# Softcap attention with a maxout expert layer: early loads in longer rows, reciprocals spread within the quad, multiplies ahead of casts

## The chip, the cores and the metric

The kernel runs on one core of a Trainium2 chip. The metric is the device time of one execution in microseconds (us). Medians are over all runs of a kernel. Ratios and intervals use fast runs.

Words used throughout: a *group* is three head pairs, the unit in which q, k and v are loaded; a *quad* is two head pairs, one turn `t` of the main loop; `i` counts head pairs, so quad `t` holds `i = 2t` and `2t + 1`. There are 48 head pairs, 24 quads and 16 groups. *Fillers* are matmuls of the expert layer which the loop hands out between the attention's instructions, a fixed number at each place.

## The reference, cut to what matters

```python
scores = q @ k^T / 8                       # 8 x 12 heads, 448 rows, 64 columns
scores = cap * tanh(scores / cap)          # cap = 30
attn   = softmax(scores)
x      = (attn @ v), heads side by side    # 3584 x 768
out    = maximum(x @ w1, x @ w2) @ w_out   # 1024 hidden columns
```

## The kernel before

`maximum(a, b) = relu(a - b) + b`, so the kernel builds `wd = w1 - w2` and `M = w2 @ w_out` (called `wm`) once, on TensorE, and computes `relu(x wd) w_out + x M`. Softmax needs no maximum because the scores are capped; each quad's sums are gathered at the end, inverted, and spread over the partitions by two DMAs, and the product with v is multiplied by them afterwards. That is the loop, for quad `t`:

```python
def pv(t, ab):                  # products with v; for ab = 1 also the sums
    ...
    nc.vector.tensor_copy(U[t][:, ab, :], ps[:, :S])
    if ab:
        nc.vector.tensor_copy(st, ss[:, :S])
        nc.sync.dma_start(out=sums[t], in_=st...)          # 7 KB
def invert(t):
    nc.vector.reciprocal(r, sums[t])
    nc.sync.dma_start(out=recd[t], in_=r)                  # 7 KB, to DRAM
def spread(t):
    for h in range(2):
        nc.sync.dma_start(out=rec[t][64*h : 64*h+64], in_=recd[t]... broadcast)   # 2 x 224 KB
def normalize(t, ab, eng=nc.gpsimd):
    eng.tensor_mul(xT[...], U[t][:, ab, :], rec[t][:, ab, :])
def cross(g):                   # groups 4 to 15: transposes q and k of a group
    nc.sync.dma_start_transpose(out=qkT_of(g)..., in_=kqf[g % 2]...)
```

All of these DMAs, and every load of q, k and v, are issued by SP (SyncE), one after the other. All multiplies and, but for most of group 0, all casts to bf16 run on GpSimd (POOL), one after the other. The order in a quad, for `t > 4`:

```python
for t in range(NQ):
    scores(t + 1, 0); ex(t, 3); ...
    spread(t - 2)                        # quad t-2's reciprocals, written in quad t-1
    extra(i)                             # loads, casts and cross of this point
    scores(t + 1, 1); ...; pv(t, 0)
    ...
    normalize(t - 2, 0); normalize(t - 2, 1)
    scores(t + 1, 2); ...
    invert(t - 1)
    extra(i + 1)                         # among others q of the odd groups
    scores(t + 1, 3); ...; pv(t, 1)      # sums of quad t
```

Of the kernel before, what the change touches and what calls it, by code (L numbers as in the profile page):

```python
# [10 lines left out]
def kernel(  # L11
# [11 lines left out]
    nc = tc.nc  # L23
# [78 lines left out]
    def rows(t, b, h0, h1):  # L102

        return t[b, h0:h1, :, :].rearrange("h (r j) d -> (h r) (j d)", j=R7)

    def raw_of(g, what):
        if (g, what) not in raw:
            raw[g, what] = stage.tile([P, 2 * L * NJ * D + (2 * L if what == "q" else L) * D], f32, name=what + "r")
        t = raw[g, what]
        m = t[:, : 2 * L * NJ * D].rearrange("p (h c) -> p h c", c=NJ * D)  # L110
        l = t[:, 2 * L * NJ * D :].rearrange("p (h d) -> p h d", d=D)
        return t, m, l

    def load(g, what, n0=0, n1=L):
        b, p = divmod(g * L, NP)
        h0, h1 = 2 * (p + n0), 2 * (p + n1)
        src = {"k": k, "q": q, "v": v}[what]
        t, m, l = raw_of(g, what)
        if g < NT and what == "v":

            x = rows(src, b, h0, h1).rearrange("(h r) c -> r h c", r=64)
            for a in range(2):
                nc.sync.dma_start(
                    out=m[64 * a : 64 * a + 64, 2 * n0 : 2 * n1, :], in_=x[:, :, NJ * D * a : NJ * D * (a + 1)]
                )
            for par in range(2):
                nc.sync.dma_start(
                    out=l[64 * par : 64 * par + 64, n0:n1, :], in_=x[:, par::2, 2 * NJ * D :]
                )
            return  # L130
        if g < NT:
            nc.sync.dma_start(
                out=t[:, n0 * S : n1 * S].rearrange("p (n c) -> p n c", c=S),
                in_=rows(src, b, h0, h1).rearrange("(n p) c -> p n c", p=P),
            )
            return
        nc.sync.dma_start(
            out=m[:, 2 * n0 : 2 * n1, :],
            in_=src[b, h0:h1, 0 : NJ * P, :].rearrange("h (p j) d -> p h (j d)", j=NJ),
        )  # L140
        if what == "q":
            nc.sync.dma_start(
                out=l[half(b), 2 * n0 : 2 * n1, :],
                in_=src[b, h0:h1, NJ * P : S, :].rearrange("h p d -> p h d"),
            )
        else:
            for par in range(2):
                nc.sync.dma_start(
                    out=l[64 * par : 64 * par + 64, n0:n1, :],
                    in_=src[b, h0 + par : h1 : 2, NJ * P : S, :].rearrange("h p d -> p h d"),  # L150
                )

    def cast(eng, g, what, n0=0, n1=L):

        b = g * L // NP
        x, m, l = raw_of(g, what)
        if what == "v":
            eng.tensor_copy(  # L158
                vp[g % 2][:, 2 * n0 : 2 * n1, :, :].rearrange("p h j d -> p h (j d)"), m[:, 2 * n0 : 2 * n1, :]
            )  # L160
            for par in range(2):
                r = slice(64 * par, 64 * par + 64)
                eng.tensor_copy(vl[g % 2][r, n0:n1, r], l[r, n0:n1, :])
            return
        if g < NT:

            x = x[:, n0 * S : n1 * S].rearrange("p (n c) -> p n c", c=S)
            if what == "q":
                eng.tensor_copy(flat(g)[:, n0:n1, Q0 : Q0 + S], x)
                return  # L170
            eng.tensor_copy(flat(g)[:, n0:n1, : NJ * P], x[:, :, : NJ * P])
            for par in range(2):
                r = slice(64 * par, 64 * par + 64)
                eng.tensor_copy(kf[g % 2][r, n0:n1, 3, r], x[r, :, NJ * P :])
            return
        o = b % 2 if what == "q" else 0
        t = (kf if what == "k" else qf)[g % 2]
        eng.tensor_copy(  # L178
            t[:, n0:n1, o : o + NJ, :].rearrange("p n j (h d) -> p n h j d", h=2),
            m[:, 2 * n0 : 2 * n1, :].rearrange("p (n h) (j d) -> p n h j d", h=2, d=D),  # L180
        )
        if what == "q":
            eng.tensor_copy(
                t[half(b), n0:n1, 3 * (1 - o), :],
                l[half(b), 2 * n0 : 2 * n1, :].rearrange("p (n h) d -> p n (h d)", h=2),
            )
        else:
            for par in range(2):
                r = slice(64 * par, 64 * par + 64)
                eng.tensor_copy(t[r, n0:n1, 3, r], l[r, n0:n1, :])  # L190
# [15 lines left out]
    def load_w2(c):  # L206
        nc.gpsimd.dma_start(out=w2b[:, c, :], in_=moe_w2[c * P : (c + 1) * P, :])
# [117 lines left out]
    def pv(t, ab):  # L325
# [21 lines left out]
                    nc.tensor.matmul(ss[32 * m : 32 * m + 32, :S], ones, x, start=False, stop=(j == nj - 1))  # L347
        nc.tensor.matmul(ps[:, :S], vl[g % 2][:, n, :], expo[t, 2][:, ab, :], start=False, stop=True)  # L348
        if ab == 0:
            U[t] = upool.tile([P, 2, S], f32, name="u", bufs=3)  # L350
        nc.vector.tensor_copy(U[t][:, ab, :], ps[:, :S])  # L351
        if ab:
            st = upool.tile([P, S], f32, name="st", bufs=1)
# [85 lines left out]
    def F(n):  # L439
        while n > 0 and fill_q:  # L440
            try:
                next(fill_q[0])
                n -= 1
            except StopIteration:
                fill_q.pop(0)
# [6 lines left out]
    def at(i, f, *a):  # L452
        todo[i].append((f, a))

    for g in range(2, NL):
        if g < NT:
            e = 0 if g == 2 else 1
            at(3 * g - 6 + e, load, g, "k")
            at(3 * g - 6 + e, load, g, "q")
            at(3 * g - 4 + e, load, g, "v")  # L460
            at(3 * g - 4, cast, nc.gpsimd, g, "k")
            at(3 * g - 4, cast, nc.gpsimd, g, "q")
            at(3 * g - 2, cast, nc.gpsimd, g, "v")
        else:
            e = 3 * g - g % 2
            at(e - 8, load, g, "k")
            at(e - 8 + g % 2, load, g, "q")
            at(e - 6, cast, nc.gpsimd, g, "k")
            at(e - 6, cast, nc.gpsimd, g, "q")
            at(e - 4, cross, g)  # L470
            at(e - 4, load, g, "v")
            at(e - 2, cast, nc.gpsimd, g, "v")
    at(1, load, 1, "v")
    at(2, cast, nc.gpsimd, 1, "v")
    for c, i in enumerate((3, 3, 4, 5, 6, 7)):
        todo[i].insert(c if i == 3 else 0, (load_w1, (c,)))
    MS = 3

    fill_const(nc.vector, 0)
    load(0, "k", 0, 1)  # L480
# [3 lines left out]
    load(1, "k")  # L484
    load(1, "q")
    load(0, "v")
    cast(nc.vector, 0, "k", 0, 1)
    cast(nc.gpsimd, 0, "q", 0, 1)
    fill_const(nc.gpsimd, 1)
    transposes(0)  # L490
    cast(nc.vector, 0, "k", 1, L)
    cast(nc.vector, 0, "q", 1, L)
# [7 lines left out]
    ex(0, 2)  # L500
    scores(0, 3)
    transposes(2)
    cast(nc.vector, 0, "v")
    cast(nc.gpsimd, 1, "k")
    cast(nc.gpsimd, 1, "q")
    for f in range(0, FC, 2):
        load_wo(f)
    for c in range(3):
        load_w2(c)
    for c in range(3, KC):  # L510
        load_w2(c)

    def weights(i):
# [9 lines left out]
    for t in range(NQ):  # L523
        i = 2 * t
        more = t + 1 < NQ
        more8 = 1 if t >= 8 and more else 0
        weights(i)
        if t % 3 == 2 and t > 2:
            fill_q.append(moe(t // 3 - 1))
        if more:  # L530
            scores(t + 1, 0)
        ex(t, 3)
        F(2)
        add(t, 0, 1)
        F(2)
        if i + 3 < NT * L:
            transposes(i + 3)
        F(5 + more8 if more else 0)
        if t > 4:
            spread(t - 2)  # L540
        extra(i)
        F(6 if more else 3)
        if more:
            scores(t + 1, 1)
            ex(t + 1, 0)
        pv(t, 0)
        F(8 + more8)
        F(3 if more else 0)
        if MS < i <= MS + KC:
            subtract(i - MS - 1)  # L550
        if t > 4:
            normalize(t - 2, 0)
            normalize(t - 2, 1)
        if more:
            scores(t + 1, 2)
            ex(t + 1, 1)
        weights(i + 1)
        if i + 4 < NT * L:
            transposes(i + 4)
        F(2 + more8 if more else 0)  # L560
        add(t, 1, 0)
        F(4 if more else 2)
        add(t, 1, 1)
        F(2 if more else 0)
        if t > 4:
            invert(t - 1)
        elif t > 1:
            spread(t - 2)
        extra(i + 1)
        F(3 + more8 if more else 0)  # L570
        if more:
            scores(t + 1, 3)
            ex(t + 1, 2)
        pv(t, 1)
        F(4)
        if more:
            add(t + 1, 0, 0)
        F(3 if more else 0)
        if 0 < t < 5:
            invert(t - 1)  # L580
        if 1 < t < 5:
            normalize(t - 2, 0)
            normalize(t - 2, 1)
        if MS < i + 1 <= MS + KC:
            subtract(i - MS)
    F(6)
    spread(NQ - 2)
    F(10)
    invert(NQ - 1)
    F(16)  # L590
    spread(NQ - 1)
# [40 lines left out]
```

## Time and profile before

| | before |
|---|---|
| median of three runs | 379.54 us (375.2 to 382.1) |
| span of the profiled run | 379.2 us |
| busy | PE 349.0, ACT 281.8, DVE 200.6, POOL 150.1 us |
| quad 0 ends at | 28.2 us |
| quads 1 to 7 | 93.8 us |
| quads 8 to 22 | 195.4 us, 12.2 to 13.4 each but one of 16.5 |
| last quad and what follows | 61.8 us |

The end of a quad is read from the copy of its sums, `st`, on VectorE in the order of time. The prediction below shows the lines of single quads. SP's own waits are listed below, with one of PE's. Columns: who waited, for whom, us in total, how often, the longest.

```profile
SPq L371 <- DMA rec_d<-rec_s: 31.4, 14, 4.4
PE s L295 <- DMA qkT<-kqf: 2.3, 2, 1.9
```

Line 371 is the spread. It waits until the reciprocals have landed in DRAM, and it waits on SP: while it does, nothing else is issued.

### The profile page before, as it was taken

What the parts mean: (1) busy time and instruction counts of PE and PEld (TensorE: products, weight loads), DVE (VectorE), ACT (ScalarE), POOL (GpSimd) and SP (SyncE); (2) the same over time, 40 slices, a digit from 0 to 9 for tenths busy, and PEclk for the clock granted to TensorE, in tenths of its full rate; (3) what the DMA queues carried; (4) which work ended last, traced back from release to release, by engine and by line L of the source; (5) the groups of instructions that cost most, each with busy time, mean ns of one, the idle gap of its engine ahead of it and who ended that gap; (6) DMA issues with size and microseconds to landing.
All of it is one profiled execution on the core that took longest, in us unless ns stands there. A gap on an engine that the chain in (4) does not pass through costs nothing.

```text
span 379.2 us, 6549 instructions
## 1 busy us (share of the span) xinstructions
PE 349.0 (92%) x2492; PEld 168.2 (44%) x2492; DVE 200.6 (53%) x348; ACT 281.8 (74%) x265; POOL 150.1 (40%) x188
## 2 busy tenths in 40 slices
PE   3677986898999999999999999999989999999996
PEld 2223443443444444444444454434434444555563
DVE  4223473567665676455745654557448556633421
ACT  4999986697999989998898899889958897000000
POOL 3734135637554445444562456243644302420000
PEclk9997898999999999999999999999989999999999
DMA  7999999996788987999698959896988132422022
GB/s 251 263 209 220 274 284 223 227 193 139 215 212 221 213 232 203 223 234 255 177 213 208 251 163 250 232 242 165 216 217 213 51 91 105 122 80 95 2 83 84
DMA packets 104464, 71.56 MB, mean 189 GB/s; under 512 B 58224, under 2 KB 99440, under 8 KB 104432
## 3 DMA queue, kind: packets, MB, share of 16 engines
q1 hardware_dynamic: 102480, 67.99, 71.1%
q0 software_dynamic: 1952, 3.15, 4.5%
q8 instruction: 19, 0.31, 0.4%
q14 instruction: 13, 0.11, 0.1%
HBM read 53.48 MB, written 11.18 MB: 171 GB/s over the span
## 4 chain that ended last, share of the span: by engine, by line
PE 65%; DMA 19%; DVE 5%; SPq 4%; ACT 3%; issue 2%; POOL 1%; POOLq 0%; DVEq 0%; ACTq 0%
PE mm L396 17%; PE mm L411 16%; PE mm L408 12%; PE pv L334 6%; DMA qkT<-kqf 6%; PE s L295 6%; DMA qr<-in_q_dram 6%; DMA vr<-in_v_dram 4%; DMA rec_b<-rec_d 3%; PE pv L348 3%; PE ss L347 2%; PE s L290 1%; DVE u L351 1%; ACT expo L303 1%; ACT tanh L296 1%
## 5 line engine op out<-in xcount | busy, mean ns | idle before, releaser
L296 ACT ACTIVATE tanh<-s 128x896 bf16<-128x896 f32 x144 | 124.3, 915 | 32.5 <-PE s L295 31.1
L303 ACT ACTIVATE expo<-tanh 128x1792 bf16<-128x1792 bf16 (+1 forms) x96 | 144.9, 1510 | 0.1
L383 POOL TENSOR_TENSOR xT<-u,rec_b 128x448 bf16<-128x448 f32 x48 | 58.4, 1238 | 101.1 <-DMA rec_b<-rec_d 81.2
L411 PE MATMUL mm<-wo_sb,gT 128*128 128x384 bf16 x448 | 86.8, 330 | 0.0
L396 PE MATMUL mm<-xT,wd_sb 128*128 128x448 bf16 x384 | 79.1, 354 | 2.7 <-POOL xT L383 1.3
L351 DVE COPY u<-pv 128x448 f32<-128x448 f32 x48 | 29.9, 624 | 91.0 <-PE pv L348 78.3
L408 PE MATMUL mm<-wm_sb,xT 128*128 128x384 bf16 x336 | 66.6, 326 | 0.2 <-DVE gT L400 0.2
L411 PEld LDWEIGHTS <-gT 128*128 128x128 bf16 x448 | 43.6, 99 | 31.1 <-issue 3.6
L415 DVE COPY osb<-mm 128x384 f32<-128x384 f32 x56 | 31.1, 555 | 46.3 <-PE mm L411 46.0
L396 PEld LDWEIGHTS <-wd_sb 128*128 128x128 bf16 x384 | 37.2, 98 | 38.4 <-issue 5.9
L295 PE MATMUL s<-qkT 64*128 64x448 bf16 x288 | 43.2, 371 | 11.1 <-ACT tanh L298 3.4
L400 DVE TENSOR_SCALAR gT<-mm 128x448 bf16<-128x448 f32 x64 | 39.1, 616 | 16.8 <-PE mm L396 16.6
L408 PEld LDWEIGHTS <-xT 128*128 128x128 bf16 x336 | 32.5, 98 | 23.3 <-issue 1.9
L334 PE MATMUL pv<-expo,vp 128*64 128x448 bf16 x288 | 37.5, 370 | 0.0
L158 POOL CAST vp<-vr 128x1152 bf16<-128x1152 f32 x15 | 18.0, 1201 | 46.8 <-DMA vr<-in_v_dram 43.5
L321 DVE TENSOR_TENSOR esum<-esum,expo 128x896 bf16<-128x896 bf16 x38 | 29.9, 787 | 1.5
L319 DVE TENSOR_TENSOR esum<-expo 128x896 bf16<-128x896 bf16 x38 | 26.6, 699 | 0.0
L295 PEld LDWEIGHTS <-qkT 64*128 64x128 bf16 x288 | 9.4, 95 | 36.8 <-issue 28.7
L298 ACT ACTIVATE tanh<-s 128x896 bf16<-128x896 f32 x24 | 22.0, 917 | 4.4 <-PE s L290 3.9
L334 PEld LDWEIGHTS <-vp 128*64 128x64 bf16 x288 | 12.4, 110 | 21.3 <-issue 15.2
L232 PE MATMUL mm<-wo_sb,w2T 128*128 128x384 bf16 x96 | 19.1, 334 | 1.4 <-DVE qkT L264 1.4
L178 POOL CAST kqf<-qr 128x1152 bf16<-128x1152 f32 x12 | 14.5, 1207 | 9.6 <-DMA qr<-in_q_dram 9.4
(56 smaller groups left out, 227.7 us busy)
## 6 DMA issues: line engine op xcount, KB each, us to landing
rec_b<-rec_d SPq DMA_DIRECT2D x48, 224.0 KB
kr<-in_k_dram SPq DMA_DIRECT2D x12, 576.0 KB
qr<-in_q_dram SPq DMA_DIRECT2D x12, 576.0 KB
vr<-in_v_dram SPq DMA_DIRECT2D x12, 576.0 KB
out_dram<-osb SPq DMA_DIRECT2D x17, 384.0 KB
out_dram<-osb SPq DMA_DIRECT2D x22, 192.0 KB
osb<-in_moe_w_dram SPq DMA_DIRECT2D x6, 512.0 KB
vr<-in_v_dram SPq DMA_DIRECT2D x8, 288.0 KB
```

What stands on the lines that cost most here:

```text
L295: nc.tensor.matmul(s[:, h, :S], k0[r, j * P : (j + 1) * P], qTn[r, :])
L296: nc.scalar.activation(tanh[t, p][:, 2 * m : 2 * m + 2, :], s[:, :, :S], AF.Tanh, scale=scale / cap)
L303: nc.scalar.activation(expo[t, p], tanh[t, p][:, 0:n, :], AF.Exp, scale=float(cap))
L321: nc.vector.tensor_add(d, d, e_of(t, ab, 0 if ab else 2))
L334: nc.tensor.matmul(ps[r, :S], vp[g % 2][:, 2 * n + h, j, :], e_of(t, ab, j)[:, h, :], start=(j == 0), stop=False)
L351: nc.vector.tensor_copy(U[t][:, ab, :], ps[:, :S])
L383: eng.tensor_mul(xT[b // 2][:, hp, cs], U[t][:, ab, :], rec[t][:, ab, :])
L396: nc.tensor.matmul(ps[:, :S], wd_sb[:, c, f * P : (f + 1) * P], x[:, c, cs], start=(c == 0), stop=(c == KC - 1))
L400: nc.vector.tensor_relu(g[:, f, cs], ps[:, :S])
L408: nc.tensor.matmul(ps[:, : DM // 2], x[:, c, ts], wm_sb[:, c, hs], start=(c == 0), stop=False)
L411: nc.tensor.matmul(ps[:, : DM // 2], g[:, f, ts], wo_sb[:, f, hs], start=False, stop=(f == FC - 1))
L415: nc.vector.tensor_copy(osb[:, hs], ps[:, : DM // 2])
```

## The change

Its intent: fill the holes of the first 98 us by loading in larger rows and in a better order, let the weights' product M and the second stage begin sooner, and free the U buffers sooner by spreading and multiplying as early as possible.

```diff
-        if g < NT and what == "v":            # v of groups 0 to 3: 4 DMAs with rows of 768 and 256 bytes
-            ... (removed; v now loads like q and k, rows of 1792 bytes, and the cast places the pieces)
-            U[t] = upool.tile([P, 2, S], f32, name="u", bufs=3)
+            U[t] = upool.tile([P, 2, S], f32, name="u", bufs=4)
 ...                                            # loads of the groups from 4 on
-            at(e - 8 + g % 2, load, g, "q")
+        at(e - 8, load, g, "q")
 ...                                            # early loads: one table of places; w2's first two
 ...                                            # chunks at the start; MS = 3 becomes 2
-        if t > 4:
-            spread(t - 2)
+        if t > 3:
+            normalize(t - 2, 0)
+            normalize(t - 2, 1)
         extra(i)
 ...
-        if t > 4:
-            normalize(t - 2, 0)
-            normalize(t - 2, 1)
 ...
+        if t == 4:
+            fill_q.append(moe(0))
 ...
+        if t > 2:
             invert(t - 1)
 ...
+        if t > 2:
+            spread(t - 1)
         pv(t, 1)
 ...                                            # fillers: 40 a quad instead of 44 up to quad 7, then 48 as before
```

More of the change, by code (lines that the diff above doesn't have):

```diff
@@ L118, in load @@
         t, m, l = raw_of(g, what)
-        if g < NT and what == "v":
-            x = rows(src, b, h0, h1).rearrange("(h r) c -> r h c", r=64)
-            for a in range(2):
-                nc.sync.dma_start(
-                    out=m[64 * a : 64 * a + 64, 2 * n0 : 2 * n1, :], in_=x[:, :, NJ * D * a : NJ * D * (a + 1)]
-                )
-            for par in range(2):
-                nc.sync.dma_start(
-                    out=l[64 * par : 64 * par + 64, n0:n1, :], in_=x[:, par::2, 2 * NJ * D :]
-                )
-            return
         if g < NT:
@@ L156, in cast @@
         x, m, l = raw_of(g, what)
+        if what == "v" and g < NT:
+            x = x[:, : L * S].rearrange("p (n c) -> p n c", c=S)
+            for h in range(2):
+                r = slice(64 * h, 64 * h + 64)
+                for a in range(2):
+                    eng.tensor_copy(
+                        vp[g % 2][64 * a : 64 * a + 64, h::2, :, :].rearrange("p n j d -> p n (j d)"),
+                        x[r, :, NJ * D * a : NJ * D * (a + 1)],
+                    )
+                eng.tensor_copy(vl[g % 2][r, :, r], x[r, :, 2 * NJ * D :])
+            return
         if what == "v":
@@ L453, in at @@
         todo[i].append((f, a))
-    for g in range(2, NL):
-        if g < NT:
-            e = 0 if g == 2 else 1
-            at(3 * g - 6 + e, load, g, "k")
-            at(3 * g - 6 + e, load, g, "q")
-            at(3 * g - 4 + e, load, g, "v")
-            at(3 * g - 4, cast, nc.gpsimd, g, "k")
-            at(3 * g - 4, cast, nc.gpsimd, g, "q")
-            at(3 * g - 2, cast, nc.gpsimd, g, "v")
-        else:
-            e = 3 * g - g % 2
-            at(e - 8, load, g, "k")
-            at(e - 8 + g % 2, load, g, "q")
-            at(e - 6, cast, nc.gpsimd, g, "k")
-            at(e - 6, cast, nc.gpsimd, g, "q")
-            at(e - 4, cross, g)
-            at(e - 4, load, g, "v")
-            at(e - 2, cast, nc.gpsimd, g, "v")
-    at(1, load, 1, "v")
-    at(2, cast, nc.gpsimd, 1, "v")
-    for c, i in enumerate((3, 3, 4, 5, 6, 7)):
-        todo[i].insert(c if i == 3 else 0, (load_w1, (c,)))
-    MS = 3
+    for g in range(NT, NL):
+        e = 3 * g - g % 2
+        at(e - 4, cross, g)
+        at(e - 8, load, g, "k")
+        at(e - 8, load, g, "q")
+        at(e - 4, load, g, "v")
+        at(e - 6, cast, nc.gpsimd, g, "k")
+        at(e - 6, cast, nc.gpsimd, g, "q")
+        at(e - 2, cast, nc.gpsimd, g, "v")
+    early = {
+        1: [(load, (1, "v"))],
+        2: [(load, (3, "k")), (load, (3, "q")), (load_w1, (0,))],
+        3: [(load_w1, (1,)), (load_w1, (2,)), (load, (2, "v"))],
+        4: [(load_w1, (3,))],
+        5: [(load_w1, (4,)), (load, (3, "v"))],
+        6: [(load_w1, (5,))],
+    }
+    for i, what in ((2, "2k"), (2, "2q"), (2, "1v"), (4, "2v"), (5, "3k"), (5, "3q"), (6, "3v")):
+        early[i].append((cast, (nc.gpsimd, int(what[0]), what[1])))
+    for i, x in early.items():
+        todo[i] += x
+    MS = 2
     fill_const(nc.vector, 0)
@@ L486 @@
     load(0, "v")
+    load(2, "k")
+    load(2, "q")
     cast(nc.vector, 0, "k", 0, 1)
@@ L489 @@
     fill_const(nc.gpsimd, 1)
+    load_w2(0)
+    load_w2(1)
     transposes(0)
@@ L502 @@
     transposes(2)
-    cast(nc.vector, 0, "v")
     cast(nc.gpsimd, 1, "k")
@@ L507 @@
         load_wo(f)
-    for c in range(3):
-        load_w2(c)
-    for c in range(3, KC):
+    for c in range(2, KC):
         load_w2(c)
@@ L527 @@
         weights(i)
-        if t % 3 == 2 and t > 2:
+        if t % 3 == 2 and t > 5:
             fill_q.append(moe(t // 3 - 1))
@@ L537 @@
             transposes(i + 3)
-        F(5 + more8 if more else 0)
-        if t > 4:
-            spread(t - 2)
+        if t == 0:
+            cast(nc.vector, 0, "v")
+        F(4 + more8 if more else 0)
+        if t > 3:
+            normalize(t - 2, 0)
+            normalize(t - 2, 1)
         extra(i)
-        F(6 if more else 3)
+        F(5 + 2 * more8 if more else 3)
         if more:
@@ L546 @@
         pv(t, 0)
-        F(8 + more8)
+        F(7 + 2 * more8)
         F(3 if more else 0)
-        if MS < i <= MS + KC:
-            subtract(i - MS - 1)
-        if t > 4:
-            normalize(t - 2, 0)
-            normalize(t - 2, 1)
+        if 3 <= i < 3 + KC:
+            subtract(i - 3)
         if more:
@@ L561 @@
         add(t, 1, 0)
-        F(4 if more else 2)
+        F(4 + more8 if more else 2)
         add(t, 1, 1)
         F(2 if more else 0)
-        if t > 4:
+        if 1 < t < 4:
+            spread(t - 2)
+        if t > 2:
             invert(t - 1)
-        elif t > 1:
-            spread(t - 2)
         extra(i + 1)
-        F(3 + more8 if more else 0)
+        F(2 + more8 if more else 0)
         if more:
@@ L578 @@
         F(3 if more else 0)
-        if 0 < t < 5:
+        if 0 < t < 3:
             invert(t - 1)
-        if 1 < t < 5:
+        if 1 < t < 4:
             normalize(t - 2, 0)
             normalize(t - 2, 1)
-        if MS < i + 1 <= MS + KC:
-            subtract(i - MS)
-    F(6)
-    spread(NQ - 2)
-    F(10)
+        if 3 <= i + 1 < 3 + KC:
+            subtract(i - 2)
+    F(16)
     invert(NQ - 1)
```

## The prediction

> **What bounds the kernel now.** I read the page first, then busy time by stage, then the end of every quad (a quad is one turn of the main loop, two head pairs; it ends with the copy of the softmax sums, `st`), then the orders of time of the engines where a quad was long.
>
> ```profile
> PE 349.0 (92%) x2492; PEld 168.2 (44%) x2492; DVE 200.6 (53%) x348; ACT 281.8 (74%) x265; POOL 150.1 (40%) x188
> PE   3677986898999999999999999999989999999996
> ACT  4999986697999989998898899889958897000000
> ```
>
> TensorE looks like the bound, and from the tenth slice on it is. But the first nine slices hold holes, and ScalarE runs out long before the end: the last sixth of the span is matmuls alone (the expert layer of the last two batches). Two bounds, then: ScalarE's tanh and exp pace the front, TensorE the back. ScalarE needs 281.8 us for 24 quads, so 11.7 us a quad.
>
> The stretches are cut at the ends of quads 0, 2, 5 and 7, around quad 20, and at the last quad. Columns: stretch, length, busy PE, PEld, DVE, ACT, POOL, clock, DMA share, GB/s.
>
> ```profile
> 0.00:28.20 28.20, 16.79 (x193) 7.30 (x194) 9.31 (x28) 21.74 (x21) 12.75 (x28) 1.00 1.00 241
> 28.20:53.20 25.00, 20.76 (x240) 9.99 (x238) 10.52 (x19) 24.70 (x24) 8.98 (x14) 0.86 1.03 263
> 53.20:98.40 45.20, 37.81 (x332) 18.28 (x330) 27.79 (x44) 34.47 (x34) 21.99 (x26) 0.96 0.91 202
> 98.40:122.00 23.60, 23.60 (x159) 11.12 (x157) 13.54 (x26) 22.81 (x22) 14.02 (x17) 1.00 0.81 205
> 122.00:275.00 153.00, 151.90 (x985) 70.72 (x983) 90.53 (x156) 140.71 (x134) 71.36 (x86) 1.00 0.89 219
> 275.00:292.00 17.00, 15.15 (x86) 6.60 (x85) 10.06 (x16) 12.29 (x12) 6.99 (x7) 0.90 0.89 225
> 324.00:379.20 55.20, 51.46 (x301) 29.25 (x299) 19.30 (x34) 0.00 (x0) 6.68 (x6) 0.99 0.23 75
> ```
>
> In 28 to 53 us ScalarE is full (24.7 of 25). In 53 to 98 it lacks 10.7 us, and TensorE 7.4: neither bound holds there, so that is where time can be won. The `st` copies start at 28.2, 41.3, 53.2, 70.5, 83.9, 98.4, 110.4 and 122.0: quads 1 to 7 took 13.1, 11.8, 17.3, 13.4, 14.6, 12.0 and 11.6 us.
>
> Quad 3, the worst, in order of time (start, length, engine, line, operation, count, idle time before it and what ended that):
>
> ```profile
> 51.45 2.12 SPq L371 DMA_DIRECT2D rec_b<-rec_d  x2
> 61.08 2.22 POOL L383 TENSOR_TENSOR xT<-u,rec_b 128x448 bf16<-128x448 f32 x2 [7.60 <-DMA rec_b<-rec_d]
> 63.33 0.62 DVE L351 COPY u<-pv 128x448 f32<-128x448 f32 x1 [5.60 <-POOL xT L383]
> 64.47 0.90 PE L262 MATMUL mm<-ident,kqf 64*64 64x64 bf16 x26 [3.66 <-DVE wm_sb L237]
> 67.98 1.73 ACT L296 ACTIVATE tanh<-s 128x896 bf16<-128x896 f32 x2 [4.26 <-PE s L295]
> ```
>
> The spread reciprocals of quad 0 were issued at 51.45 behind the k and q loads of two groups, and the multiply that needs them began at 61.08. Only then was the first of three U buffers free, so VectorE's copy waited 5.60 us; behind it, in VectorE's order, stood the eviction of a weight product, so TensorE waited 3.66 us and ScalarE 4.26.
>
> One late quad is odd, quad 20 (275.2 to 291.7, 16.5 us; its neighbours 12.2 and 13.4):
>
> ```profile
> 277.61 0.55 PE L295 MATMUL s<-qkT 64*128 64x448 bf16 x4 [1.85 <-DMA qkT<-kqf]
> ```
>
> A transposing DMA came late; the clock then fell (0.90 over 275 to 292).
>
> **What the Trainium skill says.** "Perfetto Trace Analysis", Identifying the Most-Contended Engine, warns that matmul occupancy does not tell how close to the limit the engine is. The trace agrees: in 98 to 122 PE is busy 23.60 of 23.60, though with ScalarE busy 22.81 the pace there is ScalarE's. So I take TensorE's need from long runs in the chain of waits: 48 products of line 396 in 9.08 us (0.189 each), six of line 408 in 0.97 (0.162).
>
> "DMA: Bandwidth & Descriptors", Queues, rings and completion order: on each DMA engine descriptors are consumed in ring order. The trace agrees: the 448 KB of `rec_b` issued at 51.45 took 8.61 us in the chain of waits.
>
> The same page, Rules for kernel authors, advises against two transfers to disjoint partition halves and for one 128-partition transfer. The trace shows the price on the queue: the four pieces of the first v took SP 2.51 + 2.00 us to issue, a whole k 0.40 to 0.56.
>
> "TensorE: Matmul & The Clock Gate", Part 1, says the clock halves after an idle window of about 3.4 us. Here the clock averaged 0.86 in 28 to 53 us; but a gap of 1.85 us was followed by slower products too, so a gap need not be that long.
>
> **The change, part by part.**
>
> (a) Early v loads in 1792-byte rows. In the DMA records a 256-byte packet takes 23.7 ns on the mean, one of 768 bytes 45.0, one of 1792 bytes 102. A row of v cost 2 x 45.0 + 23.7 = 113.7 ns, now 102: 384 rows over 16 engines, 0.3 us of DMA time a group, about 1 us for four. SP gains more: (4.5 + 6.9 + 2.6 + 2.8) - 4 x 0.5 = 15 us of issuing, but only the last two, some 4 us, fall where SP is behind. The cast grows from three instructions to six. GpSimd: 128x1152 takes 1.20 us, 64x384 0.573, 64x192 0.382; that line gives about 0.73 for 64x576, so 4 x 0.73 + 2 x 0.38 = 3.7 against 2.0: +1.7 us for each of three groups, beside other work. VectorE +1.3 us once. On the path: about 0.
>
> (b) Order of the early loads. Group 3's k and q move from quad 2 to quad 1, so fewer bytes precede the first spread in quad 2: 1.2 MB of k and q plus 0.5 of w1, against 1.4 + 1.2 + 0.5. At the 263 GB/s of that stretch 1.4 MB is 5 us sooner. Two w2 chunks go to the start, among the loads of k1 and q1: up to +0.5 us before quad 0 ends.
>
> (c) Spread at the end of the next quad, multiplies ahead of casts, U with four buffers. U's fourth buffer removes the 5.6 us wait: quad 4, not 3, is then the first to need quad 0's, over 11 us later.
>
> (d) M and second stage sooner, fewer fillers. Counting the program's filler calls gives 44 a quad for quads 2 to 7, now 40; from quad 8 on 48, as before. M starts one pair sooner, so quad 1 gets 25 fillers instead of 8. At the start of the tail 301 products are left before (the last row above shows just x301) and 307 after: 6 x 0.17 = +1.0 us. No product is removed.
>
> **The sum**, stretch by stretch:
> - Quad 0: 28.2, +0.5.
> - Quads 1 to 5: 70.2. At ScalarE's pace 58.7. But DMA holds this back: shares 1.00, 1.03, 0.91 over the first 98.4 us are 95 us of work at share 1; the highest share over ten microseconds was 1.15, so most of that cannot be done before 83 us, and the ideal end of quad 5 is 28.7 + 58.7 = 87.4. Waits remain; I allow 4.5 us. So 63.2: -7.0.
> - Quads 6 and 7: 23.6, at ScalarE's pace already: 0.
> - Quads 8 to 22: 195.4. TensorE's need in a quad of 48 products at 0.189 is 9.1, plus some 4.25 of attention (four score groups 1.85, products with v 1.8, sums 0.6): 13.3; in one at 0.162, 12.0. The trace shows 12.2 to 13.4, so nothing is to be won but quad 20's excess of about 3.5. Odd groups' q is now loaded with k, sooner and clear of the transposing DMA: I give that 60%, so -2.1.
> - Last quad and tail: +1.0.
>
> Together -7.6, from 379.5 to about 372. The sums lean to caution in quads 1 to 5 where (c) may help beyond quad 3, so I put the prediction at 371.
>
> **Rivals.**
> *A: DMA takes the place of the wait.* Spread now follows its reciprocal by some 2 us of program instead of half a quad, in SP's single order. SP already waited 31.4 us in total for `rec_d` before spreads; in a full queue, as in quads 2 to 4, it could block 5 us or more, delay the sums behind it and the first transposing DMA (issued at 72.6 before, 12 us ahead of its use). Also w1's first chunk is wanted at the end of quad 1 behind 1.4 MB of k and q: VectorE could stand still. For it: DMA share 1.03 to 1.15. Against: the backlog is the same bytes, sooner. Then 375 to 379.
> *B: everything fits.* Quads 1 to 5 at 11.75 and quad 20 clean: 379.5 + 0.5 - 11.5 - 3.5 + 1.0 = 366.
> *C: VectorE or GpSimd becomes the bound early.* GpSimd's +5 us stands against 22 of 45 us busy in 53 to 98: unlikely; costs 1 or 2 us.
>
> **Range and chances.** B's 366 is near the floor; below 364 TensorE would have to gain in the back, where it is full. A full rival A gives 378. The runs of before spread from 375.2 to 382.1. So 364.5 to 378. Two per cent is 371.9, in the middle of my sum: faster 0.53, within 0.44, slower 0.03.
>
> **What would show it.** Right: `u` no longer waits for the multiply in quad 3, quads 3 to 5 take 12 to 13 us, quads 8 to 19 last as before, 307 products in the tail. Quad 20 under 14 us confirms the last term. Wrong: long waits of SP before the spread; VectorE standing before the `wd_sb` subtraction or the reciprocal in quads 1 to 3; score products waiting for `qkT` at quad 5; or a slower back, which would mean that the moved fillers hurt.

## The result, and the profile after

The changed kernel is slower: median 399.31 us (398.0 to 403.0) against 378.8 us for the kernel before in the runs of that job. The ratio is 1.059, with a 95% interval from 1.048 to 1.071. Ratios here are the mean time of one kernel's fast runs over that of the other's of the same rounds, so not quite the ratio of the medians. Of the four runs of the kernel before, the ratio of 1.059 leaves out 382.09, which lies over 1.5% above the fastest and so counts as slow.

The page of the changed kernel:

```profile
PE 351.5 (89%) x2492; PEld 168.7 (43%) x2492; DVE 207.8 (52%) x351; ACT 281.7 (71%) x265; POOL 160.9 (41%) x197
PE   4677899999959999699879996999879999899996
PE mm L396 16%; PE mm L411 12%; PE mm L408 9%; DMA qkT<-kqf 8%; PE s L295 6%; DMA rec_b<-rec_d 6%; PE pv L334 5%; DMA rec_d<-rec_s 5%; DMA sums<-st 3%; PE mm L232 2%; PE pv L348 2%; ACT expo L303 2%; DMA qr<-in_q_dram 2%; ACT tanh L296 1%; PE s L290 1%
```

The second line is to be set beside its counterpart in the prediction: the first ten slices are better filled, but from the eleventh on there are 9, 5, 6, 7 and 8 where there was a row of nines with a single 8. In the third line, the chain of waits, `rec_d` (5%) and `sums` (3%) are new: tiny transfers of 7 KB now stand on the path that ends last.

Busy time by stage, cut at the ends of quads 0, 2, 5, 7 and 22 of the changed kernel (columns as in the prediction):

```profile
0.00:29.15 29.15, 17.65 (x193) 7.71 (x194) 10.74 (x30) 21.90 (x21) 17.34 (x34) 1.00 1.01 275
29.15:53.77 24.62, 20.48 (x257) 10.45 (x258) 12.54 (x21) 24.37 (x24) 9.13 (x14) 1.00 0.94 278
53.77:91.05 37.28, 34.70 (x316) 16.41 (x313) 25.00 (x41) 34.27 (x33) 22.09 (x26) 1.00 0.79 188
91.05:114.44 23.39, 22.90 (x152) 10.74 (x150) 13.52 (x24) 22.98 (x23) 10.32 (x13) 1.00 0.72 195
114.44:330.81 216.37, 196.52 (x1230) 90.48 (x1229) 119.56 (x196) 176.09 (x167) 94.98 (x107) 0.97 0.74 186
330.81:396.20 65.39, 59.23 (x351) 32.93 (x349) 26.43 (x45) 2.12 (x2) 7.05 (x6) 0.99 0.22 76
```

| stretch | before | changed | difference |
|---|---|---|---|
| quad 0 | 28.2 | 29.15 | +0.95 |
| quads 1 to 7 | 93.8 | 85.3 | -8.5 |
| quads 8 to 22 | 195.4 | 216.4 | +21.0 |
| last quad and tail | 61.8 | 65.4 | +3.6 |

So the front gained what the change was made for, and the back, in which TensorE had been full, lost more than twice that. In the back TensorE is busy 196.5 of 216.4 us, ScalarE 176 of it: neither has more work than before (191.9 and 176.0 us, at a mean clock of 0.99 where it is now 0.97).

What stands still there shows in the waits of SP and of the engines of the changed kernel:

```profile
SPq L371 <- DMA rec_d<-rec_s: 69.2, 22, 5.5
DVE rec_s L363 <- DMA sums<-st: 26.7, 9, 4.8
PE s L295 <- DMA qkT<-kqf: 16.0, 5, 4.3
```

SP's wait before the spread has more than doubled (31.4 before). VectorE stands 26.7 us before reciprocals (0.4 before), and the scores wait 16.0 us for the transposed q and k (2.3 before). How they hang together can be read from one place. First SP of the changed kernel around quad 9 (lines between these are left out):

```profile
136.67 0.53 SPq L365 DMA_DIRECT2D rec_d<-rec_s  x1
142.31 1.30 SPq L371 DMA_DIRECT2D rec_b<-rec_d  x2
143.71 0.60 SPq L357 DMA_DIRECT2D sums<-st  x1
146.19 0.60 SPq L125 DMA_DIRECT2D qr<-in_q_dram  x1
147.86 0.68 SPq L365 DMA_DIRECT2D rec_d<-rec_s  x1
152.96 1.30 SPq L371 DMA_DIRECT2D rec_b<-rec_d  x2
155.68 3.73 SPq L268 DMA_TRANSPOSE qkT<-kqf  x1
```

The write of the reciprocals goes out at 136.67, behind k and q of an even group (there before the change too). The spread stands next in SP's order and waits for it till 142.31. The sums of quad 8, copied from 132.96 on, stand behind the spread and go out at 143.71; in the kernel before they left ahead of it. The bunched q is the one at 146.19: it goes ahead of the write at 147.86, and the spread follows 5.1 us after that.

Now GpSimd and, last, TensorE in the same place (again with lines left out):

```profile
146.83 2.23 POOL L383 TENSOR_TENSOR xT<-u,rec_b 128x448 bf16<-128x448 f32 x2 [13.79 <-DMA rec_b<-rec_d]
151.69 1.15 POOL L178 CAST kqf<-kr 128x1152 bf16<-128x1152 f32 x1
155.15 0.50 POOL L183 CAST kqf<-qr 64x384 bf16<-64x384 f32 x1
162.18 0.55 PE L295 MATMUL s<-qkT 64*128 64x448 bf16 x4 [2.98 <-DMA qkT<-kqf]
```

GpSimd stood 13.79 us before the multiply. The casts behind it ended at 155.65, the transposing DMA was issued at 155.68, and TensorE waited 2.98 us for it. All three parts of the change meet here: the bunched q, the close spread and the multiplies ahead of the casts. Which of them does the harm cannot be told from this one trace. The experiments separate them.

### The profile page after: what moved, and what is told of

It is laid out like the page before. It is cut to its first block, busy times and chain, and to the rows that moved or that the text cites. A ratio compares the mean times of both kernels' runs of the same rounds, so it can differ in the third digit from the quotient of the medians.

```text
span 396.2 us, 6533 instructions
## 1 busy us (share of the span) xinstructions
PE 351.5 (89%) x2492; PEld 168.7 (43%) x2492; DVE 207.8 (52%) x351; ACT 281.7 (71%) x265; POOL 160.9 (41%) x197
## 4 chain that ended last, share of the span: by engine, by line
PE 58%; DMA 23%; DVE 7%; ACT 4%; POOL 3%; issue 2%; SPq 2%; POOLq 0%; DVEq 0%; ACTq 0%
PE mm L396 16%; PE mm L411 12%; PE mm L408 9%; DMA qkT<-kqf 8%; PE s L295 6%; DMA rec_b<-rec_d 6%; PE pv L334 5%; DMA rec_d<-rec_s 5%; DMA sums<-st 3%; PE mm L232 2%; PE pv L348 2%; ACT expo L303 2%; DMA qr<-in_q_dram 2%; ACT tanh L296 1%; PE s L290 1%
## 5 line engine op out<-in xcount | busy, mean ns | idle before, releaser
L411 PE MATMUL mm<-wo_sb,gT 128*128 128x384 bf16 x448 | 88.6, 334 | 0.0
L408 PE MATMUL mm<-wm_sb,xT 128*128 128x384 bf16 x336 | 70.4, 338 | 3.2 <-DVE osb L415 3.2
L295 PE MATMUL s<-qkT 64*128 64x448 bf16 x288 | 43.6, 372 | 23.6 <-DMA qkT<-kqf 16.0
L411 PEld LDWEIGHTS <-gT 128*128 128x128 bf16 x448 | 44.6, 100 | 32.2 <-issue 5.5
L408 PEld LDWEIGHTS <-xT 128*128 128x128 bf16 x336 | 33.4, 100 | 29.0 <-issue 8.8
L321 DVE TENSOR_TENSOR esum<-esum,expo 128x896 bf16<-128x896 bf16 x38 | 34.9, 919 | 1.1
L319 DVE TENSOR_TENSOR esum<-expo 128x896 bf16<-128x896 bf16 x38 | 28.6, 752 | 0.0
L363 DVE RECIPROCAL rec_s<-sums 32x56 f32<-32x56 f32 x24 | 11.7, 486 | 30.6 <-DMA sums<-st 26.7
L348 PE MATMUL pv<-expo,vl 128*128 128x448 bf16 x48 | 17.6, 367 | 0.0
```

Of the source, the lines that this page charges most:

```text
L295: nc.tensor.matmul(s[:, h, :S], k0[r, j * P : (j + 1) * P], qTn[r, :])
L321: nc.vector.tensor_add(d, d, e_of(t, ab, 0 if ab else 2))
L408: nc.tensor.matmul(ps[:, : DM // 2], x[:, c, ts], wm_sb[:, c, hs], start=(c == 0), stop=False)
L411: nc.tensor.matmul(ps[:, : DM // 2], g[:, f, ts], wo_sb[:, f, hs], start=False, stop=(f == FC - 1))
```

## The experiments

Fifteen kernels ran, all correct. "Back" means quads 8 to 22. Three switches of the change matter: **S**, the spread moved to the end of the quad in which its reciprocal is written; **M**, the multiplies moved ahead of the loads and casts; **Q**, q of the odd groups loaded together with k. All three are new in the changed kernel. The theories after the first look at the trace were A (M does it: GpSimd's order), B (S does it: SP's order) and C (neither: bunched loads or moved fillers).

### First job: spread and multiplies

**e1**: the multiplies back behind the casts, from quad 5 on.

```diff
-        if t > 3:
+        if t == 4:
             normalize(t - 2, 0); normalize(t - 2, 1)
         extra(i)
 ...                            # after pv(t, 0) and its fillers
+        if t > 4:
+            normalize(t - 2, 0); normalize(t - 2, 1)
```

> The changed kernel, but from quad 5 on the multiplies by the reciprocals stand again where they stood before (after the first products with v, so behind the casts of the quad). The spread stays right behind the reciprocal's write. Theory A (GpSimd's order: the multiplies wait for the late spread and hold back the casts, these the transposing DMA, this the scores): most of the loss goes, about 375 us, and score products no longer wait for qkT (16.0 us in the changed kernel, under 4 here). Theory B (SP's order: the spread waits for the reciprocal's write and holds back the sums, for which VectorE's reciprocal then stands): stays above 390 us, and VectorE still waits over 20 us before the reciprocal. Theory C (neither; the k and q loads together or the moved fillers): 395 to 400 us.

Measured: 397.61 us, ratio 1.049 (1.041 to 1.057). Theory A in its plain form missed by over 20 us.

**e2**: the spread back, the multiplies still ahead of the casts.

```diff
+        if t > 4:
+            spread(t - 2)
         if t > 3:
             normalize(t - 2, 0); normalize(t - 2, 1)
         extra(i)
 ...
-        if t > 2:
+        if t == 3:
             spread(t - 1)
```

> The changed kernel, but from quad 5 on the spread stands again early in the quad after (half a quad behind the reciprocal's write); the multiplies stay ahead of the casts, now directly behind the spread that they need. Theory A: no better than the changed kernel, 395 to 410 us, as the multiplies now always wait a whole DMA latency with the casts behind them. Theory B: the sums go out at once, VectorE's wait before the reciprocal falls from 26.7 to under 5 us, about 378 us. Theory C: 395 to 400 us.

Measured: 390.8 us, ratio 1.031 (1.024 to 1.037). VectorE's wait for the sums fell from 26.7 to 1.0 us, as B says, but the time stayed almost 13 us above B's 378.

**e3**: both back (the edits of e1 and e2 together).

> The changed kernel with both spread and multiplies back at their places of before from quad 5 on; the early loads, four U buffers, the earlier second stage, the fillers and q loaded with k remain. Theories A and B: about 372 us, quads 8 to 22 in 193 to 196 us as in the kernel before (216.4 in the changed one), quads 1 to 7 in 84 to 86 us as in the changed one. Theory C: 395 to 400 us.

Measured: 387.1 us, ratio 1.020 (1.011 to 1.030). Quads 1 to 7 took 87.2 us, as hoped; the back 207.4 against the expected 193 to 196. A and B together were not enough, and C had expected no gain at all: all three fall as they were stated, though a part of C will come back.

**e4**: the multiplies directly behind `extra(i)` instead of directly ahead of it.

> The changed kernel, but from quad 5 on each quad's multiplies come directly behind the loads and casts of the quad instead of directly ahead; nothing else moves. Theory A in its narrowest form: this swap alone takes most of the loss away, 373 to 380 us. Theory B: above 390 us. Theory C: 395 to 400 us.

Measured: 396.94 us, ratio 1.046 (1.038 to 1.054); again almost nothing.

What was left in e3 showed in its trace. Every third quad (8, 11, 14, 17 and 20) was longer than before (14.8, 18.6, 13.8, 15.3 and 18.0 us against 13.1, 12.9, 13.4, 13.1 and 16.5), and in it the scores waited for `qkT`, 11.8 us in all. Those quads need an even group's transposing DMA, and just ahead of it lies an odd group's q. SP of the kernel before, then SP of e3, at the same quad:

```profile
147.60 0.60 SPq L365 DMA_DIRECT2D rec_d<-rec_s  x1
148.24 0.49 SPq L137 DMA_DIRECT2D qr<-in_q_dram  x1
150.93 1.28 SPq L371 DMA_DIRECT2D rec_b<-rec_d  x2
152.31 5.32 SPq L268 DMA_TRANSPOSE qkT<-kqf  x1
```

```profile
145.10 0.60 SPq L125 DMA_DIRECT2D qr<-in_q_dram  x1
146.98 1.31 SPq L365 DMA_DIRECT2D rec_d<-rec_s  x1
153.20 1.30 SPq L371 DMA_DIRECT2D rec_b<-rec_d  x2
154.61 4.67 SPq L268 DMA_TRANSPOSE qkT<-kqf  x1
```

Before, the write left ahead of q and the spread followed 3.3 us later. In e3 q leaves first, the write 1.9 us after it, and the spread 6.2 us after the write. The quad had begun at 147.7 before and at 145.0 in e3, so the transposing DMA left 4.6 us into the quad before and 9.6 us in e3. All five DMAs that scores waited for in e3 left 0.1 us after the issue of the spread had ended. Hence theory D, the bunched loads of C with a path of its own: q ahead of the write delays the write, the write holds the spread, the spread holds the transposing DMA.

### Second job: the q loads

**e5**: e3, and odd q at its old place.

```diff
-        at(e - 8, load, g, "q")
+        at(e - 8 + g % 2, load, g, "q")
```

> The changed kernel with spread and multiplies back in their old places (387.1 us in the run before) and, in addition, q of the odd groups loaded again half a quad after k, so behind the reciprocal's write in SP's order. Theory D (q ahead of the write puts 576 KB in front of it in the rings; the spread, and the transposing DMA behind it in SP's order, then come later than the scores of every third quad allow): about 372 us, SP waits under 33 us for rec_d (47.0), no score products wait over 2 us for qkT (11.8 in all). Theory E (the moved fillers of the quads from 8 on, or the front, are at fault): 385 to 389 us.

Measured: 376.67 us, ratio 0.996 (0.990 to 1.001). The scores' wait fell from 11.8 to 3.3 us, the back to 194.1 us. D's direction holds. It expected 372, though: SP still waited 37.1 us for `rec_d`, not under 33. Theory E, that the moved fillers or the new front do harm, falls: they are all in this kernel, and its back is as short as that of the kernel before.

**e6**: the changed kernel with only that line old.

> The changed kernel with only the q loads of the odd groups at their old time; spread and multiplies stay new. Theory D with theory B (the spread stands close behind the reciprocal's write, about 8 us of loss on its own): between 382 and 390 us, SP's wait for rec_d well under 69.2 us, but VectorE still waits for the sums. If the bunched loads were all: about 372. Theory E: 396 to 400 us.

Measured: 393.14 us, ratio 1.040 (1.034 to 1.046); 3 us above the expected range, which had left M out as harmless; e15 will show that it is not. VectorE still waited 20.9 us for the sums.

**e7**: the kernel before with only that line new.

```diff
-            at(e - 8 + g % 2, load, g, "q")
+            at(e - 8, load, g, "q")
```

> The kernel before with one line changed: q of the odd groups is loaded together with k. Theory D: 386 to 392 us, with quads 8, 11, 14, 17 and 20 longer and the scores waiting over 8 us for qkT. Theory E: no change, 377 to 382 us. My prediction's step (q sooner is clear of the transposing DMA): 376 us.

Measured: 388.94 us, ratio 1.025 (1.019 to 1.032). The one line costs 2.5% by itself, where my prediction had credited it with 2.1 us. Its profile fell in an execution marked slow (395.1 us), so no stretch of it is read here.

**e8**: the kernel before with only the spread new, from quad 5 on.

```diff
-        if t > 4:
+        if t == 5:
             spread(t - 2)
         extra(i)
 ...
             ex(t + 1, 2)
+        if t > 4:
+            spread(t - 1)
         pv(t, 1)
```

> The kernel before with only the spread moved, from quad 5 on, to the end of the quad in which its reciprocal is written. Theory B: 385 to 390 us, SP waits for rec_d over 45 us (31.4) and VectorE waits over 10 us for the sums before reciprocals. If the spread only hurts behind the bunched loads: 377 to 382 us.

Measured: 388.1 us, ratio 1.023 (1.015 to 1.030). SP waited 47.5 us for `rec_d`, VectorE 20.6 us for the sums, both as theory B said. So S also costs 2.3% (1.5 to 3.0) alone, without bunched loads.

### Third job: which order on SP

**e9**: e5 with the transposing DMA issued ahead of the spread.

```diff
+        extra(i, True)                 # only the cross of this point
         if t > 4:
             spread(t - 2)
 ...
-        extra(i)
+        extra(i, False)                # everything else
```

> The best kernel so far (376.7 us: the changed front, spread, multiplies and odd q at their old places) with one swap: each quad's transposing DMA is issued ahead of the spread instead of behind it. If SP's order is the path (the transposing DMA waits behind a spread that waits for the reciprocal's write): the remaining 3.3 us of score products waiting for qkT and their slow clock go, 370 to 374 us. If the transposing DMA is late for other reasons (its casts, the bytes in the rings): 375 to 378 us.

Measured: 373.44 us (372.6 to 373.7, six runs), ratio 0.987 (0.982 to 0.991). This is the fastest kernel, 1.3% faster than the kernel before. Nothing waits for `qkT` any more, and the back takes 193.2 us.

**e10**: e3, so with q bunched, and the same swap.

> The same swap with q of the odd groups loaded together with k (387.1 us without the swap). If q's harm runs through SP's order alone (the write behind q, the spread behind the write, the transposing DMA behind the spread): the swap cuts that path, 371 to 376 us and under 3 us of scores waiting for qkT (11.8). If q's bytes slow the transposing DMA itself in the rings: 383 to 388 us.

Measured: 374.27 us, ratio 0.990 (0.985 to 0.995), against 387.1 without the swap; no score waits for `qkT`. This is the sharpest of the runs: the bunched q is left as it is, all its bytes are in the rings, and yet its 10 us of harm are gone. The harm thus ran through SP's order, not through the transposing DMA being slower among q's bytes.

**e11**: e6 with the spread one step later, behind the sums in SP's order.

```diff
-        if t > 2:
-            spread(t - 1)
         pv(t, 1)                       # issues the sums
+        if t > 2:
+            spread(t - 1)
```

> The changed kernel with odd q at its old time (393.1 us) and the spread moved by one step, from just ahead of the quad's last products with v to just behind them, so that the sums go out ahead of it in SP's order. Theory B (the blocked spread holds back the sums, and VectorE stands at its reciprocal): VectorE's wait for the sums falls from 20.9 us to under 5 and the time to 378 to 385 us. If the sums do not matter and the spread hurts only through what comes after: 390 to 394 us.

Measured: 393.13 us, ratio 1.037 (1.030 to 1.044). VectorE's wait for the sums fell from 20.9 to 2.5 us, exactly as B asks, but the time did not move. The scores' wait for `qkT` rose instead, from 6.8 to 15.0 us. In its trace the casts ended just as the transposing DMA was issued, with multiplies ahead of them that had waited up to 16.0 us. So M could be a second path to the same DMA, hidden in e1 and e4 by the first.

**e12**: the kernel before with four U buffers.

> The kernel before with four U buffers instead of three, nothing else. If the U buffer was the cause of the long quad 3 (17.3 us): the wait of 5.6 us of the u copy for the multiply goes, quad 3 takes 13 to 14 us, and the time falls by 2 to 5 us to about 375. If the early loads are the cause and the wait only moves on (to a later quad or to the multiply): within 1 us of before.

Measured: 376.07 us, ratio 0.994 (0.988 to 0.999). Quad 3 fell from 17.3 to 12.6 us, but quad 5 took 18.1 (14.6 before), for a new reason:

```profile
PE mm L396 <- POOL xT L383: 3.8, 2, 3.1
```

Line 396 is the second stage; it now waits for the very multiplies whose lateness had held up the U buffer. Quads 1 to 7 gained 2.1 us in all (91.7 against 93.8). The buffer alone is about a quarter of the changed kernel's 8.5; the rest belongs to the early loads, M and the fillers together, which I did not take apart.

### Fourth job: is M harmless?

**e13**: e11 with the multiplies back behind the casts.

> The changed kernel with odd q at its old time, the spread just behind the sums, and the multiplies back behind the casts (the last of these is the only difference from the run of 393.1 us). Theory F (two paths lead to the transposing DMA, over SP's order and over GpSimd's; with the first mended the second is the bound): 376 to 381 us and under 5 us of scores waiting for qkT (15.0 without). If the order on GpSimd is harmless: 390 to 394 us.

Measured: 384.49 us with one slow run among four; the three fast runs average 383.7 us, about 1.016 of the kernel before. By the fast runs, M costs 8.5 us here, though it cost 2 in e1. But 2.7 us are missing to the expected range: 7.4 us of waits for `qkT` remain, and the transposing DMAs waited for now leave 0.1 us after the spread, or after an output that follows it, in SP's order.

**e14**: M and Q old, S new.

> The changed kernel with odd q and multiplies old, the spread new and ahead of the sums. Theory F: GpSimd's path is mended, SP's stays (the reciprocal waits for sums held behind the spread): 383 to 390 us with over 15 us of VectorE waiting for the sums. If the spread hurts only through the multiplies: 376 to 379 us.

Measured: 384.5 us, ratio 1.018 (1.012 to 1.024). The scores waited only 1.1 us for `qkT`, VectorE 18.7 us for the sums: the other path by itself, as far as the waits show. SP, and the reciprocal that it made wait:

```profile
174.17 0.53 SPq L365 DMA_DIRECT2D rec_d<-rec_s  x1
179.28 1.30 SPq L371 DMA_DIRECT2D rec_b<-rec_d  x2
180.67 0.60 SPq L357 DMA_DIRECT2D sums<-st  x1
```

```profile
183.75 0.49 DVE L363 RECIPROCAL rec_s<-sums 32x56 f32<-32x56 f32 x1 [6.28 <-DMA sums<-st]
```

The spread blocks SP for 4.6 us, the sums leave at 180.67, and VectorE, whose next instructions are the copies that empty TensorE's banks, stands 6.28 us. TensorE then waited 2.69 us, till 185.76, for such a copy (`osb`). That this path makes the whole loss of S is not shown: e13 differs from e14 only in letting the sums out ahead of the spread, which ended VectorE's wait (18.7 to 2.5 us) but gained nothing (383.7 against 384.2 us, means of fast runs), as the waits for `qkT` rose from 1.1 to 7.4 us. A kernel with S, the sums first and the transposing DMA first would separate the two; it was not built.

**e15**: S and Q old, M new.

> The changed kernel with odd q and spread old, and only the multiplies still ahead of the casts (376.7 us with the multiplies old too). Theory F: GpSimd's path alone, with the multiplies waiting for a spread issued just ahead of them: 381 to 388 us, the scores waiting over 6 us for qkT. If the order on GpSimd is harmless: 376 to 378 us.

Measured: 390.09 us, ratio 1.034 (1.030 to 1.038): 13.4 us slower than e5 by M alone, more than expected. GpSimd, SP and TensorE in one such place:

```profile
270.88 2.23 POOL L383 TENSOR_TENSOR xT<-u,rec_b 128x448 bf16<-128x448 f32 x2 [14.33 <-DVE esum L321]
278.74 0.51 POOL L183 CAST kqf<-qr 64x384 bf16<-64x384 f32 x1
```

```profile
279.27 3.68 SPq L268 DMA_TRANSPOSE qkT<-kqf  x1
```

```profile
284.89 0.55 PE L295 MATMUL s<-qkT 64*128 64x448 bf16 x4 [3.53 <-DMA qkT<-kqf]
286.39 2.13 PE L408 MATMUL mm<-wm_sb,xT 128*128 128x384 bf16 x6
```

The first line's releaser is one of those that are put down to the wrong party: the multiply needed `rec_b`, for which GpSimd waited 110.7 us in this kernel (73.5 in e5). The transposing DMA left at 279.27, when the cast in front of it was done. The multiplies at 270.88 were a quad late, the casts stood behind them, and the score products waited 3.53 us. It is the same at all five waits of this kernel: the DMA leaves within 0.03 us of the last cast's end, with SP free for 2.4 to 4.9 us before. The six products after the wait took 2.13 us where six take 0.97 at full clock.

### The three switches together

Medians in us, with the front and the fillers of the changed kernel throughout:

| | spread old | spread new (S) |
|---|---|---|
| multiplies old, q old | 376.7 (e5) | 384.5 (e14) |
| multiplies old, q new (Q) | 387.1 (e3) | 397.6 (e1) |
| multiplies new (M), q old | 390.1 (e15) | 393.1 (e6) |
| multiplies new, q new | 390.8 (e2) | 399.3 (changed) |

Alone, S costs 7.8, Q 10.4 and M 13.4 us, 31.6 in sum; together they cost 22.6. The cells come from four jobs, in which the median of the kernel before went from 377.2 to 379.1; by the ratios of each job S costs 2.3, Q 2.5 and M 3.8%, all three 6.4. The delays seem to overlap because they end in the same few waits. And M beside the other two costs only 1.7 us (1.0%, with intervals that overlap): with S and Q in place, taking M away showed nothing, which had led me to drop theory A too soon. The trace of the changed kernel shows why so little could be seen. Its five transposing DMAs that scores waited for left 0.03 us or less after the last cast, but SP had been free for only 0.4 to 1.3 us then. With GpSimd out of the way, in e1 and e4, all five left 0.1 us after SP's previous issue, so SP held them almost as long.

## Why the prediction was wrong

By its own steps:

- **(a) v in longer rows, (b) order of the early loads, (d) M sooner.** Right. For quads 1 to 5 it gave 63.2 us, measured 61.9; quads 6 and 7 as before, measured 23.4 against 23.6; quad 0 +0.5, measured +0.95. The longer tail is there too: 308 matmuls run in the last 57.7 us of the changed kernel, 301 in the last 55.2 of the kernel before. The last quad and tail grew by 3.6 us instead of 1.0, but that is no miss of this step: with the spread old they take 62.8 us (e3, e5, e15), just 1.0 more than before, and 64.4 to 65.4 with it new (e1, e6, e14, changed). The rest thus belongs to S. Two inputs of these steps were slightly off: 1.2 MB for k and q of a later group leaves out their last rows (1.4 in all, but on both sides of the comparison), and the DMA share reached 1.19 over 68 to 78 us, not 1.15 at most.
- **(c) Spread, multiplies, four U buffers.** The U wait of quad 3 is gone, as told. But (c) costed nothing else. It never asked what stands behind a spread in SP's order, or behind a multiply in GpSimd's. Those two costs are S and M: 7.8 and 13.4 us alone.
- **The sum's line for quads 8 to 22.** This is the step that failed. It says "nothing is to be won but quad 20's excess" and goes on to a gain of 2.1; the runs showed +21.0. That TensorE was full there was read as protection: full, so nothing can change. It was full because the transfers just came in time. Before, the transposing DMA of an even group left 4.6 us into its quad and the scores were hardly kept waiting; quad 20, with its 1.85 us of wait, was the sign that there was no slack, and I read it as an accident to be removed.
- **Odd q "sooner and clear of the transposing DMA", -2.1 us.** Wrong in sign: +10.4 us in this kernel (e3 against e5), 2.5% on the kernel before (e7). I looked at q and the transposing DMA as two transfers in the rings. The real neighbour was the 7 KB write that q had been following, and the path ran over SP's order (e10).
- **Rival A** named the right mechanism, SP blocked by a spread too close to its write, with the delayed sums and transposing DMA behind it. It was confined to quads 2 to 4 and given 375 to 379. Those quads went well. In the back the same thing recurs in every quad.
- **Rival C** gave GpSimd 1 or 2 us for its longer casts. GpSimd did become a path, through what it waits for and not through what it has to do.

The Trainium skill has a sentence which, taken seriously, would have led there. "DMA: Bandwidth & Descriptors", Anatomy of one DMA (a section on GpSimd's path, while the DMAs here are SP's), says that DMA engines do not wait on semaphores and that any wait stands on the issuing sequencer before dispatch. The trace agrees: SP waited 69.2 us in all before line 371, with nothing issued in that time.

What stays open: how the front's 8.5 us divide among its parts beyond the U buffer; why e13 lay 2.7 us above what the theory gave; by which of the two paths, sums or transposing DMA, S does its harm; and why S, M and Q add up to less than their sum in just these amounts.

## What to carry to other kernels

Before moving a DMA that waits for another DMA, ask what stands behind it on the engine that issues it: the wait belongs to the whole queue, and here it cost about two per cent by itself (e8). The cure in such a case is order: issue first what is on the path (the transposing DMA, e9 and e10, 13 us between e3 and e10) and put the dependent transfer behind it. A fully busy engine in a profile says nothing about slack, so look for the one stretch where it does wait; and when two changes lead to the same wait, undoing either alone shows little, so undo them in all combinations before a theory is dropped.

## What the Trainium skill lacked or had wrong

- "DMA: Bandwidth & Descriptors", Rules for kernel authors, recommends to issue a DMA early and wait on its semaphore late, and in another row has a DMA that reads what an earlier one wrote wait before it is issued. It lacks what that second wait costs the DMAs queued behind it: put close behind its write, the spread cost 2.3% alone (e8), as SP's wait before it rose from 31.4 to 47.5 us.
- The same page states ring order (the 8.61 us which the prediction set beside it fit that order but do not prove it) and gives no figure for a tiny transfer behind large ones. Here a spread that needs a 7 KB write followed it by 5.6 us with k and q of a group just ahead (136.67 to 142.31, changed kernel; 5.0 us in the same place before, 138.04 to 143.01), and by 3.3 us with k ahead and q behind it (147.60 to 150.93, before).
- "TensorE: Matmul & The Clock Gate", Part 1, speaks of an idle window of about 3.4 us. In e15 a wait of 3.53 us was followed by a mean clock of 0.58 from 286 to 290 us, which agrees; before, one of 1.85 us (till 277.61) was followed by 0.52, 0.50 and 0.50 in the three us from 279 on, 0.90 over the 17 us. A single gap shorter than that window thus was enough, and it cost more than its own length: the 16.5 us quad of the kernel before held 1.85 us of waiting and was over 3 us too long.
- The pages that I read do not speak of GpSimd's order as a path between two DMAs: a multiply waiting for one transfer held back casts that another transfer needed, at 13.4 us (e15 against e5).
